# A 1x1 depthwise-separable convolution on one core: another queue for part of the weights, a wait ahead of the first load of x, and a copy behind a transpose

## The chip, the cores and the metric

The kernel runs on one core of a Trainium2 chip. The metric is the device time of one execution, in microseconds (us). Engines are named as in the profile: PE is TensorE's matmul, PEld its weight load, DVE is VectorE, ACT ScalarE, POOL GpSimd, SP SyncE; SPq and ACTq are the instructions with which SP and ACT issue DMAs.

## The reference

```python
# x: (1, 384, 384, 384), dw: (1, 1, 384), pw: (384, 384), all bf16, normal * 0.05
def reference(x, dw, pw):
    ...
    out = x * dw[0, 0][None, None, None, :]      # k = 1: one tap, no padding
    return jnp.einsum('bhwc,cd->bhwd', out, pw)
```

So every one of the 147456 pixels is a row of 384 channels, scaled by channel and multiplied by a 384 x 384 matrix. The kernel scales the matrix instead of x: it needs w = diag(dw) * pw once, and then x * w.

## The kernel before, in words

**Tiling.** The pixels are cut into 288 supertiles of 512 rows. They are loaded in chunks of 1 to 10 supertiles; the first chunks are small (1, 1, 1, 1, 2, 4 supertiles), the ones in the middle have 10. VectorE transposes a supertile in blocks of 32 x 32, taken as 32-bit words, so that a transposed block holds two channels of a pair in turn (`par` in the code). TensorE multiplies it in 48 matmuls, four at a time on the four blocks of 32 rows of the array (`tile_position`), 12 groups of four for a supertile (L230). Two halves of PSUM take turns. ScalarE copies a finished supertile from PSUM to the output buffer `Os` (L434), and SP stores it.

**The weights.** The matmul needs the scaled weights `w_r` in an order of rows that fits those pairs and blocks, repeated on all four blocks of 32 rows. They are made on the chip, in this order:
- ScalarE's queue loads `dw_row` (L183). SP loads pw's first 128 rows (L184), its last 256 rows (L185, semaphore `s_pw2`), and then x's first chunk, x0 (`load_x(0)`), and the others. L133 is the issue in `load_x`; that line serves all chunks.
- GpSimd makes an identity matrix `eye`; VectorE sums it to selection rows `sel` (L395, a `tensor_reduce`, the first sum; semaphore `s_dwf`).
- TensorE first runs matmuls on a constant (`idle_work`, L247: 16 of them, later 12), and between the two lots it turns `dw_row` into a column (L260). VectorE copies that column (L402) and makes three scaled selection matrices `sel_w` (L405).
- TensorE multiplies `sel_w` by pw in six pieces (L280), named 0 to 5 by `i = 2 * k + r`; k is the block of 128 rows of pw, so pieces 0 and 1 need pw's first 128 rows, and 2 to 5 the last 256. Pieces (k=1, r=1) and (k=2, r=0) are computed twice over.
- `w_out` (L390) copies the pieces from PSUM to `w_r`. The list `w_units` says which engine takes which: ScalarE 0, 2, one half of 3, 4 and 5; VectorE 1 and the other half of 3, the unit `(3, 1, 2, 0)`. The halves of piece 3, the fourth piece, are its two blocks of 64 channels.

After its two copies VectorE makes the transposes of the first supertile, block by block for its first three blocks (L372), then three at once (L374), as in all the others. TensorE's first main matmul waits for the first of these blocks and for the units 0 to 3 of both engines:

```python
w_first = {(0, 0): w_after(3), (4, 0): w_after(4)[1:], (4, 1): w_after(5)[1:]}
```

**Order.** Nothing is scheduled by a tool in this part. Each engine runs its instructions in the order in which the code writes them, and semaphores are waited for by hand. SP's order of loads and stores is the sorted list `todo`; a wait in it holds all that stands behind it.

Of the kernel before, what the change touches and what calls it, by code (L numbers as in the profile page):

```python
# [26 lines left out]
def kernel(  # L27
# [12 lines left out]
    nc = tc.nc  # L40
    P = nc.NUM_PARTITIONS
    B, H, W, C = x.shape
# [31 lines left out]
    pw_n = raw[:, 0 : 3 * D].rearrange("p (k d) -> p k d", d=D)  # L74
# [30 lines left out]
    s_pw2 = nc.alloc_semaphore("s_pw2")  # L105
    s_df = nc.alloc_semaphore("s_df")
    s_sw = nc.alloc_semaphore("s_sw")
    s_dwf = nc.alloc_semaphore("s_dwf")
# [4 lines left out]
    with tc.tile_critical(sync_engine=mybir.EngineType.Pool, no_gpsimd_drain=True) as section:  # L113
        def x_of(t):
            g, i, off, first, L = chunks[t]
            if first + 2 == NS:
                return Xl[:], s_xl, 32
            n = sum(len(ls) > i for ls in groups[g % NR : g + 1 : NR])
            return Xs[g % NR][:, 4 * off : 4 * (off + L), :], s_x[g % NR][i], 16 * n

        def load_x(t, eng=nc.sync):
            g, i, off, first, L = chunks[t]
            dst, sem, _ = x_of(t)
            rows = xf[512 * first : 512 * (first + L), :]
            if first + 3 < NS:
                src = rows.rearrange("(p s) c -> p (s c)", p=P)
                dst = dst.rearrange("p s c -> p (s c)")
                if i == 0 and g >= NR:
                    je = g_end[g - NR]
                    eng.wait_ge(s_t[je % 2][1], je // 2 + 1)  # L130
            else:
                src = rows.rearrange("(a k q) c -> q a k c", k=4, q=4)
            eng.dma_start(dst, src).then_inc(sem, 16)  # L133
# [48 lines left out]

        nc.scalar.dma_start(dw_row[:], dw.rearrange("a e c -> a (e c)")).then_inc(s_dw, 16)  # L183
        nc.sync.dma_start(pw_n[:, 0], pw[0:P, :]).then_inc(s_pw, 16)  # L184
        nc.sync.dma_start(pw_n[:, 1:3], pw[P:C, :].rearrange("(k p) d -> p k d", p=P)).then_inc(s_pw2, 16)  # L185
        load_x(0)

        todo = []
# [25 lines left out]
        def w_ps(i):  # L214
            return PS[0 if i in (2, 3) else 1][:, 2 * (i % 2) : 2 * (i % 2) + 2, :D]
# [132 lines left out]
        def transposes(t, j):  # L348
            g, i, off, first, L = chunks[t]
            jj = first + j  # L350
            s = jj % 2
            if jj + 1 == NS:
                nc.vector.wait_ge(s_xk, 32)
                Tw = Ts[s][:].bitcast(U32).rearrange("p b (m w) -> p (b m) w", w=32)
                for v in range(2):
                    blocks = slice(12 * v, 12 * v + 12)
                    ins = nc.vector.transpose(out=Tw[:, blocks], in_=Xk[:, blocks].bitcast(U32))  # L357
                    ins._wait_ge(s_pe, 2 * (jj - 2) + v + 1)
                    ins.then_inc(s_t[s][v])
                return  # L360
            X, sem, n = x_of(t)
            Xw = X.bitcast(U32).rearrange("p (k l) c -> p k l c", l=L)
            Tw = Ts[s][:].bitcast(U32).rearrange(
                "p b (k i) -> p b k i" if t < 2 else "p b (i k) -> p b k i", k=4
            )
            for h in range(2):
                if h == 0 and j == 0:
                    nc.vector.wait_ge(sem, n)
                if h == 0 and jj == 0:
                    for b in range(3):  # L370
                        x_b = Xw[:, :, 0, 32 * b : 32 * b + 32]
                        nc.vector.transpose(out=Tw[:, b], in_=x_b).then_inc(s_tb if b else s_t[0][0])  # L372
                    continue
                ins = nc.vector.transpose(  # L374
                    out=Tw[:, 3 * h : 3 * h + 3],
                    in_=Xw[:, :, j, 96 * h : 96 * h + 96].rearrange("p k (b w) -> p b k w", w=32),
                )
                if jj >= 2:
                    ins._wait_ge(s_pe, 2 * (jj - 2) + h + 1)
                ins.then_inc(s_t[s][h])  # L380
# [6 lines left out]
        def w_out(i, v0, v1, e):  # L387
            k, r = i // 2, i % 2
            out, in_ = w_r[:, 2 * k + v0 : 2 * k + v1, r, :], w_ps(i)[:, v0:v1]
            o = nc.vector.tensor_copy(out, in_) if e == 0 else nc.scalar.copy(out, in_)  # L390
            o._wait_ge(s_w, i + 1)
            o.then_inc(s_wr[e])
# [13 lines left out]
                sel_w[:, k], sel[:].unsqueeze(2).to_broadcast([P, 2, 4, 32]), dw_f[:, k : k + 1]  # L406
            ).then_inc(s_sw)
        for u in w_units:
            w_out(*u)
        transposes(*order[0])  # L410
        transposes(*order[1])

        for jj, (t, j) in enumerate(order):
# [29 lines left out]
            if jj + 2 < NS:  # L443
                transposes(*order[jj + 2])
# [35 lines left out]
```

## Time and profile before

| | us |
|---|---|
| runs of the kernel before | 573.43, 573.28, 573.41; median 573.41 |
| profiled execution | 573.63 |
| its span in the profile | 571.7 |
| first main matmul (L230) starts | 6.45 |
| last main matmul's stretch ends | 566.30 |

The span is the time that the profile's records cover; 573.63 is the whole execution that they were taken from. In the profile's rows the first number is the start in us from the span's start, the second the length of what is shown in the row (several instructions where it ends in x2 and more), then the engine, the line, the operation, what it writes and reads. In brackets stands how long the engine was idle before it, and what ended that.

### The profile page before, as it was taken

The page shows a single profiled execution, that of the slowest core. Times are in us where ns is not written, and L with a number is a line of the kernel's source. Part 1 is how long each engine was busy: PE and PEld are TensorE (multiplying, and loading weights), DVE is VectorE, ACT ScalarE, POOL GpSimd, SP SyncE. Part 2 cuts the span into 40 slices and gives each one's busy share as a digit, 9 for nine tenths or more (in the row PEclk, how much of TensorE's full clock was granted, in tenths as well). Part 3 has the DMA queues.
Part 4 walks back from the last instruction along what each step waited for, and adds up shares of the span by engine and source line. Part 5 has one row for each costly group of instructions (what it writes and reads, how often), then busy time and mean ns, then how long its engine had stood idle before and what let it go on. Part 6 is the DMA issues. An engine that isn't in the chain of part 4 may idle for free.

```text
span 571.7 us, 29724 instructions
## 1 busy us (share of the span) xinstructions
PE 566.9 (99%) x13847; PEld 414.4 (72%) x13847; DVE 507.9 (89%) x589; ACT 418.4 (73%) x298; POOL 13.9 (2%) x41
## 2 busy tenths in 40 slices
PE   8999999999999999999999999999999999999997
PEld 5777777777777777777777777777777777777775
DVE  7889889889889889899899898898898898898896
ACT  6777777777777777777777777777777777777775
POOL 2042000000000000000000000000000000000000
PEclk9999999999999999999999999999999999999999
DMA  8999999999999999999999999999999999998777
GB/s 320 440 385 390 434 422 429 433 421 418 421 439 414 399 405 425 403 393 393 434 387 390 408 413 404 407 411 412 406 404 415 402 395 397 423 393 330 307 286 270
DMA packets 28084, 226.88 MB, mean 397 GB/s; under 512 B 1449, under 2 KB 7850, under 8 KB 24106
## 3 DMA queue, kind: packets, MB, share of 16 engines
q1 hardware_dynamic: 27140, 225.91, 97.6%
q10 hardware_dynamic: 934, 0.89, 0.4%
q14 instruction: 9, 0.07, 0.0%
q8 instruction: 1, 0.02, 0.0%
HBM read 113.54 MB, written 113.25 MB: 397 GB/s over the span
## 4 chain that ended last, share of the span: by engine, by line
PE 99%; DVE 0%; ACT 0%; issue 0%
PE ps L230 98%; PE ps L247 0%; DVE w_r L390 0%; PE ps L315 0%; PE ps L280 0%; PE ps L303 0%; ACT O L429 0%; DVE T L372 0%; PE ps L260 0%
## 5 line engine op out<-in xcount | busy, mean ns | idle before, releaser
L230 PE MATMUL ps<-w_r,T 32*128 32x384 bf16 x13776 | 559.8, 321 | 0.3 <-DVE T L372 0.3
L374 DVE STREAM_TRANSPOSE T<-X 128x384 uint32<-128x384 uint32 x571 | 499.5, 876 | 55.2 <-DMA X<-in_x_dram 0.5
L230 PEld LDWEIGHTS ps<-w_r,T 32*128 32x128 bf16 x13776 | 411.3, 93 | 148.8 <-issue 0.9
L434 ACT CAST O<-ps 128x1536 bf16<-128x1536 f32 x286 | 411.7, 1440 | 146.6 <-PE ps L230 146.6
L344 POOL COPY Xk<-Xl 32x256 bf16<-32x256 bf16 x16 | 6.3, 396 | 0.0
L343 POOL COPY Xk<-Xl 32x128 bf16<-32x128 bf16 x16 | 4.6, 289 | 24.8 <-DMA Xl<-in_x_dram 24.0
L390 ACT CAST w_r<-ps 128x768 bf16<-128x768 f32 (+1 forms) x5 | 3.3, 754 | 1.2 <-PE ps L280 1.2
L247 PE MATMUL ps<-const-bfloat16-1.0 32*128 32x384 bf16 x28 | 2.7, 514 | 1.1 <-PEq L464 1.1
L338 POOL COPY raw<-w_r 32x768 bf16<-32x768 bf16 x4 | 3.3, 821 | 6.5 <-ACT w_r L390 6.3
L346 ACT ACT_TABLE_LOAD x1 | 1.3, 1283 | 1.5 <-PEq L464 1.5
L280 PE MATMUL ps<-raw 64*128 64x384 bf16 x16 | 2.4, 466 | 0.0
L425 DVE CAST O<-ps 128x384 bf16<-128x384 f32 x2 | 1.0, 554 | 1.4 <-PE ps L230 1.4
L280 PEld LDWEIGHTS ps<-raw 64*128 64x128 bf16 x16 | 1.0, 126 | 1.6 <-issue 1.3
L390 DVE CAST w_r<-ps 128x768 bf16<-128x768 f32 (+1 forms) x2 | 1.5, 758 | 0.7 <-PE ps L280 0.7
L247 PEld LDWEIGHTS ps<-const-bfloat16-1.0 32*128 32x128 bf16 x28 | 0.9, 121 | 1.6 <-issue 1.4
L374 DVE STREAM_TRANSPOSE T<-Xl 128x384 uint32<-128x384 uint32 x2 | 1.8, 882 | 0.2
L395 DVE TENSOR_REDUCE sel<-eye 128x64 f32<-128x128 bf16 x1 | 0.3, 289 | 1.5 <-POOL eye L325 1.5
L357 DVE STREAM_TRANSPOSE T<-Xk 128x384 uint32<-128x384 uint32 x2 | 1.2, 578 | 0.5 <-PE ps L230 0.4
L429 ACT CAST O<-ps 128x384 bf16<-128x384 f32 x2 | 1.0, 480 | 0.7 <-PE ps L315 0.7
L315 PE MATMUL ps<-raw,T 128*128 128x384 bf16 x8 | 1.5, 328 | 0.0
L429 DVE CAST O<-ps 128x384 bf16<-128x384 f32 x2 | 1.1, 558 | 0.1
L424 ACT CAST O<-ps 128x384 bf16<-128x384 f32 x2 | 0.9, 482 | 0.5 <-PE ps L230 0.5
(14 smaller groups left out, 5.1 us busy)
## 6 DMA issues: line engine op xcount, KB each, us to landing
X<-in_x_dram SPq DMA_DIRECT2D x25, 3840.0 KB, 21.8
out_dram<-O SPq DMA_DIRECT2D x25, 3840.0 KB, 27.7
X<-in_x_dram SPq DMA_DIRECT2D x3, 1536.0 KB, 18.5
X<-in_x_dram SPq DMA_DIRECT2D x2, 1920.0 KB, 14.5
out_dram<-O SPq DMA_DIRECT2D x2, 1920.0 KB, 24.0
out_dram<-O SPq DMA_DIRECT2D x2, 1536.0 KB, 13.0
X<-in_x_dram SPq DMA_DIRECT2D x6, 384.0 KB, 5.8
out_dram<-O SPq DMA_DIRECT2D x3, 768.0 KB, 5.7
```

Source lines behind the costliest of these rows:

```text
L230: mm = nc.tensor.matmul(PS[s][:, q, :D], lhsT=Ts[s][32 * q : 32 * q + 32, b, par::2], rhs=w_r[32 * q : 32 * q + 32, b, par, :], start=(b, ...
L247: nc.tensor.matmul(PS[0][:, 2 * (i % 2) + i // 2, :D], lhsT=ones[32 * i : 32 * i + 32, 0:P], rhs=ones[32 * i : 32 * i + 32, :], start=True ...
L280: mm = nc.tensor.matmul(PS[(k + 1) % 2][:, 2 * r + v, :D], lhsT=sel_w[64 * v : 64 * v + 64, k, r, :, :].rearrange("p q w -> p (q w)"), rhs ...
L315: mm = nc.tensor.matmul(PS[1][:, m, :D], lhsT=Tk[:, P * (m + 2) : P * (m + 3), par], rhs=w_k[:, par, :], start=False, stop=par == 1,)
L338: nc.gpsimd.tensor_copy(w_k[quads[n]], w_r[quads[n], n]).then_inc(s_wk)
L343: nc.gpsimd.tensor_copy(Xk[quads[n], g:8:4, :], x_b).then_inc(s_xk)
L344: nc.gpsimd.tensor_copy(Xk[quads[n], 8 + g : 24 : 4, :], Xl[quads[g], :, 64 * n : 64 * n + 64]).then_inc(s_xk)
L346: nc.scalar.copy(warm[:, s : s + 1], nc.const_aps.tensor(0.0, [P, 1], F32)).then_inc(s_a[s])
L374: ins = nc.vector.transpose(out=Tw[:, 3 * h : 3 * h + 3], in_=Xw[:, :, j, 96 * h : 96 * h + 96].rearrange("p k (b w) -> p b k w", w=32),)
L390: o = nc.vector.tensor_copy(out, in_) if e == 0 else nc.scalar.copy(out, in_)
L429: o = (nc.scalar.copy if n % 2 else nc.vector.tensor_copy)(Ov[:, n, j, :], PS[s][:, n, :D])
L434: a = nc.scalar.copy(Ov[:, :, j, :], PS[s][:, :, :D])
```

## The change

ScalarE's queue, behind `dw_row`, issues the load of pw's last 256 rows, and SP's queue no longer does. SP waits for VectorE's first sum before it issues x's first chunk. VectorE's half of the fourth piece comes out of the list before the transposes and is copied behind the first block's transpose of the first supertile.

```diff
         nc.scalar.dma_start(dw_row[:], dw.rearrange("a e c -> a (e c)")).then_inc(s_dw, 16)
         nc.sync.dma_start(pw_n[:, 0], pw[0:P, :]).then_inc(s_pw, 16)
-        nc.sync.dma_start(pw_n[:, 1:3], pw[P:C, :].rearrange("(k p) d -> p k d", p=P)).then_inc(s_pw2, 16)
+        nc.scalar.dma_start(pw_n[:, 1:3], pw[P:C, :].rearrange("(k p) d -> p k d", p=P)).then_inc(s_pw2, 16)
+        nc.sync.wait_ge(s_dwf, 1)
         load_x(0)
 
@@ transposes(t, j)
                     for b in range(3):
                         x_b = Xw[:, :, 0, 32 * b : 32 * b + 32]
                         nc.vector.transpose(out=Tw[:, b], in_=x_b).then_inc(s_tb if b else s_t[0][0])
+                        if b == 0:
+                            w_out(3, 1, 2, 0)
                     continue
 
@@
         for u in w_units:
-            w_out(*u)
+            if u[:2] != (3, 1):
+                w_out(*u)
         transposes(*order[0])
         transposes(*order[1])
```

## The prediction

> **What bounds the kernel now.** I read the page first, for its span and its costliest group, and then the chain of waits, in order of time, because a change to the opening of a kernel counts only where it moves the first instruction of the long stretch.
>
> ```profile
> span 571.7 us, 29724 instructions
> L230 PE MATMUL ps<-w_r,T 32*128 32x384 bf16 x13776 | 559.8, 321 | 0.3 <-DVE T L372 0.3
> ```
>
> ```profile
> 1.12 1.47 PE ps L247 x14
> ...
> 2.60 0.18 PE ps L260
> ...
> 2.84 0.98 PE ps L247 x7
> 3.82 0.77 PE ps L280 x4
> 4.59 0.03 issue
> 4.62 0.96 DVE w_r L390
> 5.58 0.00 issue
> 5.58 0.56 DVE w_r L390
> 6.13 0.23 DVE T L372
> 6.36 0.09 issue
> 6.45 559.85 PE ps L230 x13776
> ```
>
> The 13776 main matmuls run in one piece for 559.85 us from 6.45 us on, with 0.3 us of idle time ahead of them in all. Four of them make a group (one for each block of 32 rows), so 559.85 / 3444 = 0.163 us a group, and nothing in the diff touches that. What the diff can move is the start at 6.45. The chain into it is: the warm-up matmuls (L247, L260), the first two pieces of the weights (L280), VectorE's copy of piece 1 (0.96 us), its half of piece 3 (0.56 us), the first transpose T0 (0.23 us up to where its successor starts), a hand-over of 0.09 us. So the forecast is the time before plus the shift of 6.45, plus any new gap right behind it. About 0.2%, 1.15 us here, is what a measurement of this kernel can tell from no change; the start would have to move by a sixth of itself for that.
>
> **The issues.** The timeline of the opening shows the queues, and the views of the single lines how long each load took to land, counted from its issue.
>
> ```profile
> 0.96 0.39 SPq L184 DMA_DIRECT2D raw<-in_pw_dram  x1
> 0.97 0.54 ACTq L183 DMA_DIRECT2D dw_row<-in_dw_dram  x1
> 1.41 0.41 SPq L185 DMA_DIRECT2D raw<-in_pw_dram  x1
> 1.48 0.29 DVE L395 TENSOR_REDUCE sel<-eye 128x64 f32<-128x128 bf16 x1 [1.48 <-POOL eye L325]
> 1.54 1.28 ACT L346 ACT_TABLE_LOAD   x1 [1.54 <-PEq L464]
> 1.88 0.46 SPq L133 DMA_DIRECT2D X<-in_x_dram  x1
> 2.84 0.28 ACT L346 COPY warm<-const-float32-0.0 128x1 f32<-128x1 f32 x2
> 24.26 0.42 ACTq L137 DMA_DIRECT2D Xl<-in_x_dram  x1
> ```
>
> SP loses the issue of pw's last 256 rows (0.41 us), so it would be free for x's first chunk x0 at 1.41. The new wait holds x0 until VectorE's sum ends at 1.48 + 0.29 = 1.77. With a hand-over between 0.03 and 0.09 us (the two in the chain above) x0 is issued at 1.80 to 1.86, against 1.88: 0.02 to 0.08 us earlier. Behind that wait on SP stand x's other chunks and all stores; they move with it, by as little. I book the two edits on SP together at nothing.
>
> On ScalarE the load of pw's rows goes in behind dw_row, at 0.97 + 0.54 = 1.51, so 0.10 us later than on SP. Its issue costs 0.42 us by the one other plain load of that queue (L137). The table load and the two small copies slide by that: the copies end at 2.84 + 0.28 + 0.42 = 3.54. The first thing they would hold up is ScalarE's first copy out of PSUM at 4.30 (below), so 0.76 us of cover remain; the edit costs nothing there. dw_row itself is issued as before, ahead of the moved load.
>
> **The data of the two loads.** This is where the unknown lies. Before, both loads stood on one queue, pw's rows ahead of x0. Now they stand on two, and x0 starts on its own queue before pw's rows are through.
>
> ```profile
> DMA to landing us min/median/max: 2.5/2.5/2.5
> DMA to landing us min/median/max: 3.7/3.7/3.7
> DMA to landing us min/median/max: 5.3/5.3/5.3
> ```
>
> ```profile
> 2.00:3.00 1.00, 0.98 (x19) 0.29 (x15) 0.12 (x1) 0.99 (x3) 0.00 (x0) 1.00 0.70 165
> 3.00:3.90 0.90, 0.90 (x14) 0.26 (x8) 0.86 (x4) 0.12 (x2) 0.00 (x0) 1.00 1.06 281
> 3.90:5.58 1.68, 1.68 (x12) 0.74 (x10) 1.01 (x3) 1.28 (x2) 0.00 (x0) 1.00 0.99 305
> ```
>
> The three landings are those of L185 (issued 1.41), of x0 (1.88) and of x's second chunk x1 (issued 0.50 us after x0, at 2.38). So pw's rows landed at 1.41 + 2.5 = 3.91, x0 at 5.58 and x1 at 7.68. The last columns of the three stretches are the share of the DMA engines and GB/s: from 3 us on the engines are full. In the new order the same bytes are moved, so x0 lands no later than about 5.58, unless x1 cuts in; what can change is the share. For pw's rows the bounds are: landing after their own 2.5 us, 1.51 + 2.5 = 4.01, if x0 takes nothing from them; or together with x0, 5.58, if the two are dealt out evenly and x0's longer rows take most of the time. I take a value near the lower end, 4.0 to 4.4: they are issued 0.3 us ahead of x0 and it was their turn first before as well. But both ends stay in the range.
>
> [...]
>
> **What a late landing costs.** Rows of the pieces of the weights:
>
> ```profile
> 4.05 0.15 PEld L280 LDWEIGHTS ps<-raw 64*128 64x128 bf16 x2 [0.17 <-DMA raw<-in_pw_dram]
> 4.37 0.53 PE L280 MATMUL ps<-raw 64*128 64x384 bf16 x2
> 4.69 0.53 PE L280 MATMUL ps<-raw 64*128 64x384 bf16 x2
> 5.01 0.53 PE L280 MATMUL ps<-raw 64*128 64x384 bf16 x2
> 5.82 0.33 PE L280 MATMUL ps<-raw 64*128 64x384 bf16 x2
> 4.30 0.80 ACT L390 CAST w_r<-ps 128x768 bf16<-128x768 f32 x1 [1.18 <-PE ps L280]
> 4.99 0.80 ACT L390 CAST w_r<-ps 128x768 bf16<-128x768 f32 x1
> 5.68 0.50 ACT L390 CAST w_r<-ps 128x384 bf16<-128x384 f32 x1
> 6.05 0.30 DVE L372 STREAM_TRANSPOSE T<-X 128x128 uint32<-128x128 uint32 x1
> 6.66 0.54 DVE L374 STREAM_TRANSPOSE T<-X 128x384 uint32<-128x384 uint32 x1
> 7.70 7.68 DVE L374 STREAM_TRANSPOSE T<-X 128x384 uint32<-128x384 uint32 x10 [0.50 <-DMA X<-in_x_dram]
> ```
>
> The weight load at 4.05 is the first to use the moved rows, its matmuls (piece 2) come at 4.37 and end at 4.90; piece 3 follows at 4.69 and 5.01 and ends at 5.54. A weight load needs 0.15 us, so a landing up to about 4.37 - 0.15 = 4.22 costs nothing at all. Beyond that pieces 2 and 3 slide, and ScalarE with them: its copy of piece 2 (4.99), then of its half of piece 3 (5.68 to 6.18). The first main matmul waits for that half too, and 6.18 lies 0.18 us ahead of the 6.36 at which the chain leaves VectorE. So the landing is free until about 4.22 + 0.18 = 4.40, half a microsecond later than before, and past that each 0.1 us costs 0.1 us at the start. At the upper end, 5.58, that makes 5.58 - 4.40 = 1.18 us.
>
> **VectorE's order.** T0 and the half of piece 3 change places: before 0.96, 0.56, T0; now 0.96, T0, 0.56. The sum is the same, and the start waits for both in either order, so as a swap it costs nothing. What it changes is which of the two may be late. T0 now wants x0 at 5.58, where before it came at 6.05, so the old cover of 0.47 us for x0 is gone: x0's landing at 5.58 is just in time, and each 0.1 us later costs 0.1 us. With T0 from 5.60 (x1 landed at 7.68 and its transpose began at 7.70), the half copy from 5.83, its end at 6.39 and 0.09 us of hand-over the start is 6.48: +0.03 us. In return piece 3 may come at 5.83 rather than 5.58, 0.25 us of new cover on VectorE; ScalarE, which takes the other half at 5.68, limits what that is worth. T1 and T2 slide with the copy by about the same 0.03, and the first main matmuls use two groups per transposed block, 2 x 0.163 = 0.33 us, against 0.23 us between transposes, so nothing stops there.
>
> Behind the start there is one more narrow place. The second supertile's transpose began at 7.70, when x1 landed, and 48 matmuls after 6.45, at 6.45 + 12 x 0.163 = 8.41, TensorE wants it. Its first half takes 0.54 us, by the half of the first supertile at 6.66 (the same form), so it was there at 8.24, with 0.17 us to spare. x1's bytes come last in either order, so I book nothing, and 0.1 us either way in the range.
>
> **Sum.** Profiled execution before 573.63 us (span 571.7 and 1.93 around it); shift +0.03 from VectorE's order, about 0 from the issues, 0 from pw's rows up to a landing of 4.40, and 0 at the end, where nothing is changed. That gives 573.66 for a profiled run. The profiled run stands 0.22 us over the median of the runs, 573.41, so the median is forecast at 573.44; with 0.05 for an x0 that is a little late, 573.5.
>
> **The rivals.**
> 1. *It stays as summed* (chance 0.50): landing of pw's rows up to 4.40, x0 near 5.58; 573.3 to 573.7, with 573.5 the likeliest. Part of this case is that the change hardly does what it says: the wait opens at 1.77, so x0 goes out when it went before.
> 2. *pw's rows share with x0* (0.30): they land at 4.7 to 5.5, TensorE waits in front of piece 2, ScalarE's half of piece 3 becomes the last wait: +0.3 to +1.1 us, 573.7 to 574.5. An even share from 2.9 on doubles the 1.1 us that were left to 4.01, which is a landing at 5.1 and +0.7 us. For it: the engines are full from 3 us on. Against it: the head start.
> 3. *TensorE stays slow* (0.14, slower by over 0.2%). The pairs of L280 start 0.32 us apart at 4.37, 4.69 and 5.01 and take 0.53 us; the last takes 0.33, and the main groups follow at 0.163: the array came to full pace at about 5.7, some 4.6 us after its first matmul at 1.12, and it had hardly paused till then. If pw's rows land at 5.1, TensorE pauses from 4.6 to 5.1 in that stretch. If such a pause starts the count again, full pace comes at 5.1 + 4.6 = 9.7; the start is at 6.45 + 0.7 = 7.15, and 2.55 us at half pace lose 1.3 us; with the 0.7 that is +2.0 us, 575.4. [...] The profile's granted clock is 1.00 throughout and so cannot tell it. [...]
> 4. *Faster* (0.06): both loads together finish earlier, or dw_row, which released the matmul at 2.60 and so the whole chain, lands earlier; 573.0 to 573.3, since the chain from 2.60 on is arithmetic and copies. For more than 0.2% it would have to start at 5.3, before VectorE is through with piece 1 (5.58), or save in the 1.93 us outside of the span, of which the profile shows nothing; that is 0.04 of these 0.06.
>
> Case 1 and 2 are within 0.2% but for the end of 2 (a landing past 5.55; 0.02). So slower 0.16, same 0.80, faster 0.04. The range: from 573.1, below case 1, to 574.5, the upper end of case 2; case 3, the end of case 2 and the larger part of case 4 are left out, 0.14 + 0.02 + 0.04 = 0.2.
>
> **What would show it.** In the changed profile: x0's issue at 1.80 to 1.86; pw's rows on ScalarE's queue at 1.51 with a landing under 4.40; TensorE's L280 pairs without a pause after 4.05; T0 at 5.6, the half copy behind it, and the first main matmul at 6.48. A pause ahead of piece 2 is case 2, and a first main group of 0.3 us is case 3. A wait of T0 for x0 well past 5.6, or of the second supertile for x1, would make the sum wrong at VectorE's order.

## The result, and the profile after

| | before | after |
|---|---|---|
| median of 9 runs, us | 573.69 | 576.11 |
| lowest to highest, us | 573.28 to 575.55 | 574.72 to 576.96 |
| profiled execution, span, us | 573.63, 571.7 | 576.01, 574.0 |

The ratio is 1.0038, with a 95% interval of 1.0024 to 1.0051: the changed kernel is slower by 0.38%, 2.2 us. The forecast was 573.5 with a range up to 574.5; the time lies above the range, near the case *TensorE stays slow* (575.4), which had a chance of 0.14.

The page of the profile after:

```profile
span 574.0 us, 29724 instructions
L231 PE MATMUL ps<-w_r,T 32*128 32x384 bf16 x13776 | 560.5, 321 | 0.0
L281 PE MATMUL ps<-raw 64*128 64x384 bf16 x16 | 2.9, 517 | 1.7 <-DMA raw<-in_pw_dram 1.7
```

Its chain of waits (start, length, what):

```profile
1.54 4.49 DMA raw<-in_pw_dram
6.03 0.05 issue
6.08 2.10 PE ps L281 x12
8.18 560.47 PE ps L231 x13774
```

Lines above 184 are one to four higher than before: the main matmul is L231, the pieces of the weights L281. The chain no longer goes through VectorE. It goes from the issue of pw's last 256 rows on ScalarE's queue (1.54) to their landing at 6.03, then through the twelve matmuls that need them, then straight into the main stretch. Both views name the same wait: 1.7 us of TensorE in front of piece 2, released by the load of pw.

The timeline of the same stretch shows what became of each step:

```profile
1.54 0.41 ACTq L185 DMA_DIRECT2D raw<-in_pw_dram  x1
1.79 0.34 SPq L133 DMA_DIRECT2D X<-in_x_dram  x1
3.28 0.28 ACT L347 COPY warm<-const-float32-0.0 128x1 f32<-128x1 f32 x2
4.09 0.80 ACT L393 CAST w_r<-ps 128x768 bf16<-128x768 f32 x1 [0.53 <-PE ps L281]
5.88 0.31 DVE L373 STREAM_TRANSPOSE T<-X 128x128 uint32<-128x128 uint32 x1 [0.51 <-DMA X<-in_x_dram]
7.01 0.53 PE L281 MATMUL ps<-raw 64*128 64x384 bf16 x2
7.65 0.53 PE L281 MATMUL ps<-raw 64*128 64x384 bf16 x2
8.41 0.53 PE L231 MATMUL ps<-w_r,T 32*128 32x384 bf16 x4
8.73 0.53 PE L231 MATMUL ps<-w_r,T 32*128 32x384 bf16 x4
9.65 0.49 PE L231 MATMUL ps<-w_r,T 32*128 32x384 bf16 x8
```

The pairs of the pieces stay 0.32 us apart (7.01, 7.65 with one between them) up to the last, and so do the first main groups (8.41, 8.73), until about 9.6. The length of the rows drops below 0.53 there. Before, the array had been at full pace from 5.7.

That gives the sum. The span grew by 2.3 us. The start moved from 6.45 to 8.18, +1.73; the main stretch from 559.85 to 560.47, +0.62. Three experiments below in which the pieces ran at full pace needed 1.70 us from the first of these matmuls to the start, where this profile needs 2.10. So in this profile, of the 1.73, 0.40 belong to the slow array and 1.33 to the late rows; late rows 1.33, slow array 0.40 + 0.62 = 1.02.

### The profile page after: what moved, and what is told of

It reads as the page before. It is cut to its first block, busy times and chain, and to the rows that moved or that the text cites. A ratio compares the mean times of both kernels' runs of the same rounds, so it can differ in the third digit from the quotient of the medians.

```text
span 574.0 us, 29724 instructions
## 1 busy us (share of the span) xinstructions
PE 567.9 (99%) x13847; PEld 343.0 (60%) x13847; DVE 510.4 (89%) x589; ACT 418.6 (73%) x298; POOL 13.9 (2%) x41
## 4 chain that ended last, share of the span: by engine, by line
PE 98%; DMA 1%; ACTq 0%; ACT 0%; issue 0%; POOLq 0%
PE ps L231 98%; DMA raw<-in_pw_dram 1%; PE ps L281 0%; PE ps L316 0%; PE ps L304 0%; ACTq L183 0%; ACT O L433 0%; ACTq L479 0%; POOLq L113 0%; POOLq L468 0%
## 5 line engine op out<-in xcount | busy, mean ns | idle before, releaser
L231 PE MATMUL ps<-w_r,T 32*128 32x384 bf16 x13776 | 560.5, 321 | 0.0
L231 PEld LDWEIGHTS ps<-w_r,T 32*128 32x128 bf16 x13776 | 340.0, 93 | 220.8 <-issue 1.1
L281 PE MATMUL ps<-raw 64*128 64x384 bf16 x16 | 2.9, 517 | 1.7 <-DMA raw<-in_pw_dram 1.7
L281 PEld LDWEIGHTS ps<-raw 64*128 64x128 bf16 x16 | 0.9, 127 | 3.7 <-DMA raw<-in_pw_dram 3.0
```

The lines of the kernel that those rows point to most:

```text
L231: mm = nc.tensor.matmul(PS[s][:, q, :D], lhsT=Ts[s][32 * q : 32 * q + 32, b, par::2], rhs=w_r[32 * q : 32 * q + 32, b, par, :], start=(b, ...
L281: mm = nc.tensor.matmul(PS[(k + 1) % 2][:, 2 * r + v, :D], lhsT=sel_w[64 * v : 64 * v + 64, k, r, :, :].rearrange("p q w -> p (q w)"), rhs ...
```

## The experiments

Each kernel was timed in several runs, or ran once with the profiler. The ratios are to runs of the kernel before that were made beside it; their medians are 573.50 to 573.92. The starts and lengths are those of one profiled run, which need not be a typical one: that of e3 is its fastest (574.15), that of e2 its slowest (577.48). "Landed" is the issue plus the time to landing of pw's last 256 rows.

| kernel | landed | main stretch starts, lasts | median (runs), us | ratio, 95% interval |
|---|---|---|---|---|
| before (profile above) | 3.9 | 6.45, 559.85 | 573.69 (9) | 1 |
| changed kernel | 6.03 | 8.18, 560.47 | 576.11 (9) | 1.0024 to 1.0051 |
| e1_queue_back | 3.9 | 7.00, 559.83 | 573.95 (10) | 0.9998 to 1.0017 |
| e2_order_back | 6.30 | 8.45, 561.71 | 576.53 (4) | 1.0032 to 1.0066 |
| e3_no_x_wait | 5.02 | 6.77, 559.83 | 575.36 (6) | 1.0020 to 1.0046 |
| e14_no_wait_again | 5.74 | 7.88, 560.27 | 575.48 (1) | |
| e5_fill_pause | 5.8 | 8.24, 559.83 | 576.55 (4) | 1.0028 to 1.0061 |
| e11_fill_five | 6.28 | 8.03, 559.83 | 575.39 (6) | 1.0020 to 1.0046 |
| e6_pause_only | 3.8 | 8.12, 560.13 | 575.86 (4) | 1.0027 to 1.0061 |
| e4_x_after_pw | 4.16 | 8.40, 561.43 | 577.31 (1) | |
| e10_x_later | 4.2 | 7.26, 561.51 | 576.09 (1) | |
| e7_pw_long_rows | 6.07 | 8.22, 560.30 | 575.84 (1) | |
| e8_x_short_rows | 4.67 | 6.79, 559.83 | 573.93 (1) | |
| e12_pw_short_rows | 6.40 | 8.55, 561.67 | 577.54 (1) | |
| e9_swap_queues | 5.97 | 8.11, 561.63 | 577.23 (1) | |
| e13_x1_held | 5.74 | 7.49, 561.51 | 576.52 (1) | |

### Which of the three edits

**e1_queue_back.** Only the move to ScalarE's queue undone.

```diff
-nc.scalar.dma_start(pw_n[:, 1:3], ...).then_inc(s_pw2, 16)
+nc.sync.dma_start(pw_n[:, 1:3], ...).then_inc(s_pw2, 16)
```

> Only the move to ScalarE's queue is undone; the wait ahead of x0 and VectorE's new order stay. Theory (the move alone makes pw's rows late, because x0 then runs beside them): pw's rows land at about 3.9 to 4.0 us, TensorE does not pause ahead of piece 2, the main matmuls start at 6.4 to 6.6, and the time is that of before within 0.3 us. Rival (the wait or VectorE's order costs something of its own): the start stays at 7 or later, or the time 1 us or more above before.

The loss is gone: 573.95, an interval that holds 1. TensorE does not pause and the main stretch is all at full pace. The start, though, is 7.00 and not 6.4 to 6.6. The chain of waits of this kernel says why:

```profile
1.87 4.09 DMA X<-in_x_dram
5.97 0.02 issue
5.99 0.31 DVE T L373
6.30 0.46 DVE w_r L393
6.76 0.24 issue
7.00 559.83 PE ps L231 x13776
```

and its timeline the idle time ahead of T0:

```profile
5.99 0.31 DVE L373 STREAM_TRANSPOSE T<-X 128x128 uint32<-128x128 uint32 x1 [0.68 <-DMA X<-in_x_dram]
```

Here x0 landed at 5.97 instead of 5.58, VectorE stood 0.68 us in front of T0 with the half copy of piece 3 queued behind it, and the start slid with it. The cover that the new order gives away is really missing: in this profile the start came 0.55 us later than before. It does not show clearly in the median.

**e2_order_back.** Only VectorE's new order undone (the half copy ahead of T0 again).

> Only VectorE's new order is undone: the half of piece 3 stands ahead of the first transpose again; the queue move and the wait stay. Theory: pw's rows land at about 6.0 as in the changed kernel, piece 3 ends at 7.2, and now T0 comes behind the half copy instead of ahead of it, so the start is 0.2 to 0.3 us later than 8.12, and the time that much above the changed kernel's 576.1. Rival (the new order is part of the loss): the start comes back towards 6.5 and the time falls by 0.5 us or more.

The intervals of this kernel and the changed one overlap, so the order is no part of the loss that can be told. The 0.2 to 0.3 us that T0 behind the copy should have cost did not appear either: the start comes 2.10 us after the first late matmul (6.35 to 8.45), as in the changed kernel (6.08 to 8.18). While the array is slow, TensorE's own pieces 4 and 5 are the last thing ahead of the start, and VectorE's order lies in their shadow. This profile's long main stretch (561.71) comes from the array alone: its groups stay at the slow pace until about 12.4.

**e3_no_x_wait, e14_no_wait_again.** Only the wait ahead of x0 taken out.

```diff
-nc.sync.wait_ge(s_dwf, 1)
 load_x(0)
```

> The changed kernel without the wait ahead of x0, so x0 is issued at about 1.41, ahead of pw's last 256 rows at 1.54. Theory (the two loads and x1 take turns, and a lead of 0.3 us decides little): pw's rows land at 6.0 to 6.6, start 8.1 to 8.7, time within 0.5 us of the changed kernel's 576.1. Rival (the wait does protect pw's rows, or costs something itself): landing at 7 or more and 577 or more; or a time 0.6 us or more below the changed kernel.

> A second profile of the kernel without the wait ahead of x0. Theory (x0 ahead of pw's rows is through before they start, so they meet x1 only): landing at 4.8 to 5.4 again, against 5.8 to 6.3 in the four profiles with the wait. Rival (the one early landing was chance): 5.8 or later.

The chain of waits in e3:

```profile
1.53 3.49 DMA raw<-in_pw_dram
5.02 0.05 issue
5.07 0.35 PE ps L280 x2
...
6.77 559.83 PE ps L230 x13776
```

The first profile has pw's rows at 5.02, the second at 5.74. The median of e3 is 0.75 us under the changed kernel's, with overlapping intervals, and the one run of e14 0.6 under. So neither the expectation (6.0 to 6.6, then 4.8 to 5.4) nor a firm gain: what stands is that the wait did not protect pw's rows. With it they landed at 5.8 to 6.3 in four profiles whose loads are the same (the changed kernel, e2, e5, e11), without it at 5.0 and 5.7.

### Why the rows come late

**e4_x_after_pw, e10_x_later.** x0's issue waits for pw's rows (`s_pw2` at 16), or for VectorE's copy of dw's column (`s_dwf` at 2).

> The changed kernel, but x0 is issued only when pw's last 256 rows have landed, so that these are alone with pw's first 128. Theory (they are late because x0 and x1 run beside them): landing 2.3 to 2.6 us after the issue, at about 4.0, no pause ahead of piece 2; x0 issued at 4.1 lands at 6.5 to 7.5 and becomes the last wait. Rival (a load on ScalarE's queue is slow in itself): landing at 5 or later though nothing runs beside it.

> The changed kernel with x0's issue held until VectorE has copied dw's column, at about 2.85 instead of 1.79. Theory (pw's rows are late only by what x0 takes beside them): they land at 4.1 to 4.6, TensorE hardly pauses, but x0, issued 1.06 us later, lands at 6.4 to 7.0, and T0 behind it sets the start at 7.0 to 7.6. Rival (x0's late issue still lets it overtake): pw's rows land at 5.5 or later.

The chain of waits of e4 has the load by itself:

```profile
1.54 2.62 DMA raw<-in_pw_dram
```

Alone, ScalarE's queue lands the rows 2.62 us after the issue, against 2.5 on SP's: it is not a slow queue. With x0 issued at 2.86 (e10) they still land after 2.7. So they are late by x0's load when it is issued 0.25 us behind theirs (1.79 against 1.54 in the changed kernel, 6.03), and hardly when it is issued 1.32 us behind (e10). Both kernels then start late on x0, as expected (8.40, 7.26).

**e9_swap_queues.** pw's rows back on SP, x0 on ScalarE's queue.

> The two loads change queues: pw's last 256 rows are issued by SP behind its first 128, as in the kernel before, and x0 by ScalarE behind dw_row, at about 1.5; VectorE's order stays. Theory (any two loads on two queues take turns): pw's rows still land late, at 5.0 to 5.6, since x0's 8 pieces per engine are dealt in between, but not as late as in the changed kernel, as x1 stands behind pw on SP's queue. Rival (ScalarE's queue comes second to SP's): pw's rows land at about 4.0 and x0 at 6 or later.

The same step in the chain of e9:

```profile
1.41 4.56 DMA raw<-in_pw_dram
```

Late again, at 5.97, now on the queue on which they landed at 3.9 before. In these runs it is not a matter of which queue, but of both loads at once: 5.97 and 6.03 with x0 on the other one, against 3.9 with both on one (before) and 4.16 with x0 held (e4). It is later than the theory's 5.0 to 5.6.

**e8_x_short_rows, e7_pw_long_rows, e12_pw_short_rows, e13_x1_held.** The first has x0 in pieces of 768 bytes instead of 3072; the second pw's rows in pieces of 1536, the third in 384 instead of 768; in the fourth x1's issue waits for `s_pw2`. The first three bring x's or pw's rows in another order and so compute another output; they move the same bytes, and only their times are read here.

> The changed kernel with x0 in pieces of 768 bytes instead of 3072, four to a partition from four places (the rows of the first supertile come out permuted). Theory (piece by piece in turn): each turn of x0 is a quarter as long, so pw's rows land at 4.4 to 5.2, and x0 lands later than in the changed kernel, at 6 or more. Rival (share by bytes or by lots): pw's rows within 0.3 us of 6.0.

> The changed kernel with pw's last 256 rows laid out two rows to a partition, so that the same 192 KB are 128 pieces of 1536 bytes instead of 256 of 768 (the weights come out permuted). Theory (the DMA engines take the two queues in turn piece by piece, so that 16 pieces per engine of pw wait for some 8 of x0 and then some of x1): with 8 pieces per engine they wait for fewer of x's and land at 4.6 to 5.4 instead of 6.0. Rival (the engines share by bytes, or take large lots in turn): landing within 0.3 us of 6.0.

> The changed kernel with pw's last 256 rows loaded as 512 pieces of 384 bytes (half rows, which stand permuted in the weights). Two to a piece of before did nothing (6.07), four short pieces for one of x0's brought the landing to 4.67. Theory (turns piece by piece, twice as many turns now): landing at 7.0 or later. Rival (what counts is the size of the other queue's pieces and not the number of pw's own): landing at 5.8 to 6.4.

> The changed kernel with x's second chunk held until pw's last 256 rows have landed, so that only x0 runs beside them. Theory (on some of the DMA engines pw's pieces take turns with x's long ones for as long as there are any, x1's after x0's): without x1 pw's rows land at 5.0 to 5.5 instead of 5.8 to 6.3. Rival (x0 alone holds them up): 5.8 or later.

x0's piece size made a good deal of difference: with short pieces pw's rows landed at 4.67 instead of 6.03 (and x0 no later, T0 came at 5.79), the array lost nothing in the main stretch, and the one run took 573.93, against 573.50 for the kernel before beside it. The size and number of pw's own pieces moved the landing little: 6.07 and 6.40 around 6.03; so my theory of strict turns, piece for piece, falls on both. For e12 that is less than it seems: its issue took 0.71 us instead of 0.41, none of its packets moved before 4.25 (17 by 4.5), and from 4.5 to 5.0 the queue then moved 334 packets against 20 of x's. x1's part is small: 5.74 without it, where 5.0 to 5.5 was expected.

The queues of the changed kernel show how it looks from the DMA engines. Each pair of rows is one half microsecond, 2.5, 3.0, 4.0 and 4.5 us (packets, MB, share of 16 engines); q10 is ScalarE's queue, q1 SP's:

```profile
q10 hardware_dynamic: 48, 0.04, 81.0%
q1 hardware_dynamic: 13, 0.00, 3.5%
...
q10 hardware_dynamic: 50, 0.04, 35.3%
q1 hardware_dynamic: 4, 0.01, 7.9%
...
q1 hardware_dynamic: 57, 0.17, 84.5%
q10 hardware_dynamic: 39, 0.03, 15.8%
...
q1 hardware_dynamic: 65, 0.19, 94.0%
q10 hardware_dynamic: 18, 0.01, 7.4%
```

For comparison e4, where x0 waits, from 2.5 and from 3.0:

```profile
q10 hardware_dynamic: 30, 0.02, 46.5%
q1 hardware_dynamic: 12, 0.00, 3.4%
...
q10 hardware_dynamic: 165, 0.13, 76.5%
```

The first half microsecond is slow on this queue in either case, 48 packets or 30 of the 272 that the trace counts for the load (256 rows and 16 more), and does not by itself make the rows late. Two things add up behind it. From 3.0 to 3.5 the queue moves 50 packets in the changed kernel, against 165 with x0 held; yet x0 has moved only 4 by then, and all the packets together take 43% of the engines' time. Then x0 comes in number, and from 4.0 on the last 75 packets trickle out beside it with a 15th to a 6th of the engines' time. So the even share that the prediction priced was generous. Why the rows hardly move at 3.0, before x0's data do, the trace does not show. By which rule an engine picks between the queues stays open: the trace has no rows by engine, and neither strict turns nor shares by bytes fit all four runs (4.67, 6.07, 6.40, 5.74).

### The slow array

**e6_pause_only.** The kernel before, with a pause and nothing else.

```diff
 nc.tensor.wait_ge(s_pw2, 16)
+nc.tensor.wait_ge(x_of(0)[1], 16)
```

> The kernel before, its queues and order untouched, but TensorE waits for x0 as well ahead of piece 2, which makes a pause from about 4.4 to 5.6 us. Theory (a pause of about a microsecond is enough to keep the array slow): pairs 0.32 us apart behind the pause, start at about 7.7, main groups at 0.32 us until 9 or later: +1.25 us for the start and +0.5 to +1.2 behind it, 575.2 to 576. Rival (the array comes to full pace at 5.7 whatever it does in the pause): pairs at 0.16 us, start at 7.0 to 7.2, no slow main group, +0.6 to +0.8 us.

The chain of waits in e6, from the end of piece 1 on:

```profile
4.37 1.65 issue
6.02 2.10 PE ps L281 x12
8.12 560.13 PE ps L230 x13776
```

With queues and order of before, a pause of 1.65 us in front of piece 2 gives the loss of the changed kernel: 575.86, 1.0027 to 1.0061. The pieces behind it take 2.10 us, all at 0.32 a pair, as expected; the start is later than expected by 0.4, as x0 landed at 5.97 here. The slow array shows in the runs too: at full pace (1.70 us) the start behind this pause would be 7.72, 1.3 us later than before, and all four runs lie 1.8 us or more over the kernel before beside them (573.72).

**e5_fill_pause, e11_fill_five.** The changed kernel with six, then five, groups of constant matmuls in the pause.

```diff
 if k == 1:
+    idle_work(6)      # e11: idle_work(5)
     nc.tensor.wait_ge(s_pw2, 16)
```

> The changed kernel with six more groups of constant matmuls between pieces 1 and 2, so that TensorE works through its wait for pw's rows. Theory (the pause keeps the array slow): pw's rows land at about 6.0 as before this edit; the array is at full pace by 5.5 to 6, so pieces 2 to 5 run 0.16 us apart instead of 0.32 and the main groups at 0.163 from the first; start at 7.3 to 7.7, main stretch 559.9 instead of 560.5, time 1.0 to 1.4 us below the changed kernel. Rival (the array's pace has nothing to do with the pause): the pairs stay 0.32 us apart up to about 9.4 and the time stays within 0.3 us of the changed kernel.

> As with six groups of constant matmuls between pieces 1 and 2, but five, so that they end at about 5.9 and don't outlast the wait for pw's rows (six of them ended at 6.4 where the rows had come at 5.84). Theory (without a pause the array comes to full pace somewhere between 4.1 and 6.9, and the late landing costs the rest): main stretch 559.8, start at 7.4 to 8.1, time 575.0 to 575.8, 0.3 to 1.1 below the changed kernel. Rival (the pace does not hang on the pause): a main stretch of 560.3 or more, time as of the changed kernel.

Six groups outlasted the load, as they ran at the slow pace (24 matmuls in 2.10 us): piece 2 began at 6.34, half a microsecond after the rows, and the time stayed at 576.55; the expectation for the time missed. The main stretch, though, was 559.83, without one slow group. Five groups fit; the timeline of e11 and the last step of its chain:

```profile
6.32 0.76 PEld L282 LDWEIGHTS ps<-raw 64*128 64x128 bf16 x12 [1.41 <-DMA raw<-in_pw_dram]
6.32 1.15 PE L282 MATMUL ps<-raw 64*128 64x384 bf16 x12 [1.02 <-DMA raw<-in_pw_dram]
```

```profile
8.03 559.83 PE ps L231 x13776
```

The rows landed even later than in the changed kernel, at 6.28, yet the pieces took 1.15 us instead of 2.10 and the start came 1.71 us behind the first of them. 575.39 is 0.7 us under the changed kernel's median; the two intervals overlap, so a gain is seen in the trace and not in the times. In this profile a pause of 1.02 us remained and the array kept its pace. It had reached it before: the five groups themselves took 1.00 us from 4.30 on, full pace from the first. So the fill did not bring the pace here, and e3 and e13, without a fill, ran their pieces at full pace too, behind pauses of 0.70 and 1.44 us. That filling the pause helps is not shown.

When it is lost after it had been reached, the granted clock shows it. Windows of TensorE in e13 (length, busy time and count, granted clock, DMA share, GB/s):

```profile
6.00:7.00 1.00, 0.93 (x12) 1.00 0.32 34
7.00:8.00 1.00, 0.51 (x8) 0.79 0.79 270
8.00:9.00 1.00, 1.00 (x17) 0.50 1.02 381
10.00:11.00 1.00, 1.00 (x20) 0.50 0.92 218
11.00:12.00 1.00, 1.00 (x32) 1.00 0.86 323
```

After idle times of 1.44 and 0.55 us the granted clock falls to 0.50 at 7.6 and is back at 1.00 at 11.0. That is a stretch of 3.4 us. e4 and e10 show the same 0.50 for as long: by the clocks of their windows from 8.3 to 11.7 and from 7.6 to 11.0.

When the array first comes to full pace differs from profile to profile. By the spacing of the pairs, and by the first record of the granted clock, which stands at the same moment in the traces of before (5.65) and after (9.61; the views read 1.00 ahead of it, slow or not), it was at 4.1 to 5.1 us in e1, e3, e4, e10, e11 and e13, 5.7 before, 6.2 in e8, 7.2 in e5, 8.8 to 9.6 in e6, e14, e7 and the changed kernel, and 11.9 to 12.4 in e9, e2 and e12. The pause's length does not tell these apart: 1.39 us (e9) and 1.41 (e14) left the pieces slow, 1.44 (e13) did not. In three of the ten profiles with a pause of 0.7 us or more the pieces behind it ran at full pace, twelve matmuls in 1.15 us (e3, e11, e13): e11 had it from 4.30 on, e13 by the end of piece 1 at 4.35, and e3 shows it from 5.07 on, with the first matmul behind its pause. The other seven took 2.10 us and came to full pace at 8.8 or later. Up to 4.1 us the changed kernel and e13 run the same instructions of TensorE at the same times, within 0.01 us; that the moment falls early in one and late in the other is not the kernel's doing.

## Why the prediction was wrong, point by point

- **Bound and place: right.** All of the 2.3 us in the span is the shift of the first main matmul plus slow groups right behind it.
- **The issues: right.** x0 went out at 1.79 (1.80 to 1.86 was said), pw's rows at 1.54 with 0.41 us (1.51, 0.42), the small copies on ScalarE ended at 3.56 (3.54), ahead of its first copy at 4.09.
- **The step that failed: the landing of pw's rows.** "I take a value near the lower end, 4.0 to 4.4: they are issued 0.3 us ahead of x0." They landed at 6.03, past even the upper bound of 5.58. The head start that decided the choice was worth nothing: beside an issued x0 the rows moved 50 packets from 3.0 to 3.5, where 165 moved with x0 held. The bound failed too, because it took x0's landing in one profile, 5.58, for the latest at which both loads are through; here x0 itself let T0 start only at 5.88.
- **The price of a late landing: right in form, and its size came near by luck.** Free to 4.40 and then one for one gives 6.03 - 4.40 = 1.63 for a landing at 6.03; the start moved by 1.73. At full pace the same landing would have cost 1.33, and the slow pieces added 0.40, which the price did not hold. The last wait was not ScalarE's half of piece 3, as priced, but TensorE's own pieces 4 and 5 at the slow pace.
- **TensorE stays slow: right in what was seen, too small a chance.** Case 3 named the pause ahead of piece 2, pairs at 0.32 us and slow main groups, full pace at 9.7, and +2.0 us. Measured: about 9.6, and +2.3 in the span. That these lie so close is luck: the landing was taken at 5.1 and came at 6.03, the slow pace was to lose 1.3 us behind the start and lost 0.62 there. Its count from the end of the pause was wrong: without a pause the array came to full pace at 4.1 (e1), 5.7 (before) and 7.2 (e5), so no count of 4.6 us is shown; the moment moved from profile to profile, from 4.1 to 12.4 us in all. And "granted clock 1.00 throughout and so cannot tell" holds only for the views of the opening: a clock that is lost later is shown (0.50).
- **VectorE's order: right that it costs the cover of x0.** e1 has T0 waiting for x0 until 5.97. That x0 lands at 5.58 "just in time" was one profile; in others T0 came behind its wait for x0 at 5.83 (e5), 5.88 (the changed kernel), 5.99 (e1) and 6.13 (e11).
- **x1: no loss of its own.** The main stretch has 0.0 us of idle time ahead of it.

## What to carry to other kernels

Here two loads that are needed one after the other were better off on one queue in that order (the small one landed at 3.9 before and in e1): on a second queue it landed 2.1 us later beside the large one, at 6.03, though it was issued 0.25 us ahead of it. In an opening that is as tight as this one, look at what TensorE would do while it waits, not only at the wait: behind a pause of 1.7 us the changed kernel lost another 1.02 us at half pace, and the same kernel can lose more or less, as the moment of full pace shifts from run to run (e3 and e14 are one kernel: full pace by 5.07 in the one profile, at 8.8 in the other). And where a landing in one profile is "just in time", take its spread over several before giving away the work that covered it.

## What the runs showed of the hardware that was not expected

pw's rows on a second queue did not merely share with x0's load: in the half microsecond from 3.0 the whole core's DMA moved 98 GB/s, where it moved 250 with x0 held (e4) and 324 before, on one queue. Alone on that queue the load took 2.62 us, beside x0 4.3 to 4.8 in the four profiles with the same loads. And the size of the *other* load's pieces (3072 against 768 bytes) moved its landing by 1.4 us, while its own (384 to 1536) moved it by 0.4 at most, with the late start of e12 in it.

Where a trace shows the clock lost and regained (e4, e10, e13), half clock (0.50) lasted 3.4 us. It came behind an idle time of 1.51 us in front of the main stretch in e10; behind one of 1.29 us in e1 it did not come.

Part of the spread of the changed kernel's nine runs goes with the array's clock: mean granted clock 0.997 in the four runs at 576.45 to 576.96, 0.999 or 1.000 in the five at 574.72 to 576.11. 0.003 of 574 us is 1.7 us, half of the 3.4 us at 0.50 that e4, e10 and e13 show; these three read 0.997 too. In the profile of the changed kernel the step from 1.000 to 0.999 lies behind the last matmul and costs no work: TensorE is through at 570.7, and the clock falls to 0.50 at 572.8. And the mean does not hold the slow opening: the profile of e2 reads 1.000 with the longest main stretch of all.
